# Moving fold blocks, a turned tile, the first output and the norm chain in the program order of a cross-covariance and expert kernel

## The chip, the cores and the metric

One NeuronCore of a Trainium2 chip. The metric is the device time of one execution in microseconds (us), the median of several runs. All runs quoted here were in the same undisturbed ("fast") state.

## The reference

Two stages, four batches of 6080 rows of 256:

```python
qn = q / (np.linalg.norm(q, axis=1, keepdims=True) + 1e-06)
kn = k / (np.linalg.norm(k, axis=1, keepdims=True) + 1e-06)
s = kn.transpose(0, 2, 1) @ qn / tau           # 256 x 256 per batch
a = np.exp(s - s.max(-1, keepdims=True)); a /= a.sum(-1, keepdims=True) + 1e-09
x = v @ a                                       # (24320, 256)
h = x @ w_in                                    # d_ff = 2048
r = np.maximum(h, 0.0)
out = (moe_s * (r * r) + moe_b) @ w_out
```

## The kernel before

Per batch the kernel makes a 256 x 256 matrix of scores on TensorE, divides by column norms, takes exponentials, and *folds* the result into w_in (`wa`). So h is v times `wa`, and the tokens pass through in 48 groups (47 of 512, the last of 256). A group has 16 *steps*; a step is one block of 128 hidden columns, two matmuls of 512 columns. All else is hung on a step by number (`at_step`), and every engine works strictly in that order. Between the h matmuls of group g stand the output matmuls of group g-1 (seven products in place of eight, 128 columns each), and, in batch b-1's groups, the scores and norms of batch b.

```python
# end of a batch, one item per at_step: norms (sqrt on ACT), recip (DVE: S/norm), turn (transposes),
# exps (ACT, with a table load), sums (row sums), then the folds into w_in
def scaled(f0, n, m, wa_ps):                    # half 0 on ACT, half 1 on DVE
    dst = self.wa[:, m, ds(f0, n)]
    if m == 0:
        po(nc.scalar.mul(out=dst, in_=wa_ps, mul=st["rs"][:, m : m + 1]))
    else:
        po(nc.vector.tensor_scalar_mul(out=dst, in0=wa_ps, scalar1=st["rs"][:, m : m + 1]))
# ... (cut)
if self.b == 0:
    folds = [fold_both(0, NW // 2), fold_both(NW // 2, NW // 2)]     # NW = 512
# ... (cut)
for i in range(NPIECE + 1):
    at_step(11 + i, lambda i=i: rowconst_sum(i))     # DVE sums of w_out, from DMA pieces
at_step(23, rowconst_mm)                             # ones x sums in the PSUM tile of the scores, then DVE
# ... (cut)
if g == 1:
    at_step(12, lambda g=g: transpose_v(g))          # turn v of group 1 on TensorE, copy on DVE
# ... (cut)
for b in range(1, B):
    w0 = first_group[b - 1] * FT + (26 if b == 1 else 6)      # first step of batch b's scores
    w1 = first_group[b] * FT - 3
    fin_len = 5 * 3 + 8 * 2                                   # the end starts this many steps ahead
    span = (w1 - fin_len) - w0 - 8
    n = NCH * JC                                              # 12 chunks of 4 row blocks
    for c in range(NCH):
        sc = w0 + span * c * JC / n
        # ... (cut: loads, 4 x 2 score matmuls)
        # norms of a chunk: square on ACT, square on DVE, two sums of halves on DVE
        for i, f in enumerate(ops):
            at_step(int(sc) + 2 + 1 + i * 2, f)
# ... (cut)
PLAG = {0: 14, NG - 1: 5}        # output of group 0 runs 14 steps behind its h
```

There is one PSUM tile for scores and folds, two for h, three for outputs. *rowconst* is a row that every output gets (the column sums of w_out times moe_b). Its product stands in the PSUM tile of the scores, so the first scores of batch 1 wait until DVE has read it.

Of the kernel before, what the change touches and what calls it, by code (L numbers as in the profile page):

```python
# [16 lines left out]
def kernel(  # L17
# [13 lines left out]
    P = 128  # L31

    B, N, C = q.shape
# [11 lines left out]
    CH = C // P  # L45
    FT = Dff // P
    TG = 512
    NG = (NT + TG - 1) // TG
# [5 lines left out]
    def po(ins):  # L54

        tc.keep_in_program_order(ins)
        return ins
# [30 lines left out]
    def h_tile(name):  # L88
        return ps_h.tile([P, 2, TG], FP32, tag="h_ps", name=name)
# [19 lines left out]
    class Gram:  # L109
# [105 lines left out]
        def finish_ops(self):  # L215

            st = {}

            def norms():
                self.add_norms(last=True)  # L220
                nrm = sm_pool.tile([P, 2, CH], FP32, tag="nrm", name="nrm")
                po(nc.scalar.activation(out=nrm, in_=self.n_ps, func=AF.Sqrt))  # L222
                st["nrm"] = nrm

            def recip():
                nrm = st["nrm"]
                po(nc.vector.tensor_scalar_add(out=nrm, in0=nrm, scalar1=EPS))
                st["r"] = sm_pool.tile([P, 2, CH], FP32, tag="rnrm", name="rnrm")
                po(nc.vector.reciprocal(out=st["r"], in_=nrm))
                if inv_tau != 1.0:  # L230
                    po(nc.vector.tensor_scalar_mul(
                        out=st["r"][:, 0], in0=st["r"][:, 0], scalar1=inv_tau))
                st["s"] = sm_pool.tile([P, CH, C], FP32, tag="sm_s", name="sm_s")
                po(nc.vector.tensor_mul(
                    st["s"], self.s_ps, st["r"][:, 1, :, None].broadcast_to((P, CH, C))))

            def turn():
                st["t"] = self.bank("t_ps", CH, C)
                for j in range(CH):
                    for ch in range(CH):  # L240
                        po(nc.tensor.transpose(
                            st["t"][:, j, ts(ch, P)], st["s"][:, ch, ts(j, P)], ident32))

            def exps():
                st["e"] = sm_pool.tile([P, CH, C], FP16, tag="eT", name="eT")
                for j in range(CH):
                    po(nc.scalar.activation(
                        out=st["e"][:, j, :], in_=st["t"][:, j, :], func=AF.Exp,
                        scale=st["r"][:, 0, j : j + 1]))
                self.wa = apool.tile([P, CH, Dff], FP16, tag="wa16", name="wa16")  # L250

            def sums():
                r_ps = self.bank("r_ps", CH, C)[:, :, 0]
                for ch in range(CH):
                    for j in range(CH):
                        po(nc.tensor.matmul(r_ps[:, ch : ch + 1], st["e"][:, j, ts(ch, P)],
                                            ones16[:, 0:1], start=(ch == 0 and j == 0),
                                            stop=(ch == CH - 1 and j == CH - 1),
                                            skip_group_check=True))
                st["rs"] = sm_pool.tile([P, CH], FP32, tag="rs", name="rs")  # L260
                po(nc.vector.tensor_scalar_mul(out=st["rs"], in0=r_ps, scalar1=1.0 / LAM))
                po(nc.vector.reciprocal(out=st["rs"], in_=st["rs"]))

            def scaled(f0, n, m, wa_ps):
# [4 lines that stand above are left out]
                    po(nc.vector.tensor_scalar_mul(  # L269
                        out=dst, in0=wa_ps, scalar1=st["rs"][:, m : m + 1]))  # L270

            def fold_mm(f0, n, m, wa_ps):
                for j in range(CH):
                    po(nc.tensor.matmul(wa_ps, st["e"][:, j, ts(m, P)],  # L274
                                        w_in16[:, j, ds(f0, n)],
                                        start=(j == 0), stop=(j == CH - 1)))

            def fold_both(f0, n):
                def f():
                    wa_ps = h_tile("wa_ps")  # L280
                    for m in range(CH):
                        fold_mm(f0, n, m, wa_ps[:, m, :n])
                    for m in range(CH):
                        scaled(f0, n, m, wa_ps[:, m, :n])
                return f

            def fold_one(f0, n, m):
                def f():
                    wa_ps = self.bank("wa_ps", CH, C).rearrange("p a c -> p (a c)")
                    fold_mm(f0, n, m, wa_ps)  # L290
                    scaled(f0, n, m, wa_ps)
                return f

            if self.b == 0:

                folds = [fold_both(0, NW // 2), fold_both(NW // 2, NW // 2)]
            else:
                folds = []
            folds += [fold_one(f0, NW, m) for f0 in range(NW if self.b == 0 else 0, Dff, NW)
                      for m in range(CH)]  # L300
            return [norms, recip, turn, exps, sums] + folds
# [8 lines left out]
    def group(g):  # L310
        t0 = g * TG
        return t0, min(TG, NT - t0) // P
# [3 lines left out]
    def load_v(g):  # L316
        t0, nj = group(g)
        v16 = vpool.tile([P, TG // P, C], FP16, tag="v16", name="v16")
        po(nc.gpsimd.dma_start(  # L319
            out=v16[:, :nj, :],  # L320
            in_=v_flat[t0 : t0 + nj * P, :].rearrange("(p j) c -> p j c", j=nj)))
        v_tiles[g] = v16

    def transpose_v(g):
        _, nj = group(g)
        v16 = v_tiles.pop(g)
        vT_ps = ps_h.tile([P, CH, TG], FP16, tag="h_ps", name="vT_ps")
        for j in range(nj):
            for ch in range(CH):
                po(nc.tensor.transpose(vT_ps[:, ch, ts(j, P)], v16[:, j, ts(ch, P)], ident16))  # L330
        vT = vtpool.tile([P, CH, TG], FP16, tag="vT", name="vT")
        po(nc.vector.tensor_copy(out=vT[:, :, : nj * P], in_=vT_ps[:, :, : nj * P]))
        vT_tiles[g] = vT
# [29 lines left out]
    NW = 512  # L363
# [49 lines left out]
    fin = g0.finish_ops()  # L413
# [2 lines left out]
    keep_busy(5, w_in16[:, 0, :P], w_in16[:, 0, :NW])  # L416
    fin[2]()
    transpose_v(0)
    for f in fin[3:7]:
        f()  # L420


# [32 lines left out]
    def at_step(s, f):  # L455
        side.setdefault(int(s), []).append(f)

    first_group = [b * N // TG for b in range(B)]
    for i, f in enumerate(fin[7:]):
        at_step(i // 2 * 4 + i % 2 + 1, f)  # L460
    at_step(14, lambda: po(nc.vector.tensor_scalar_mul(
        out=s_out, in0=s_bc, scalar1=1.0 / (LAM * LAM))))
    for i in range(NPIECE + 1):
# [5 lines left out]
    for g in range(NG):  # L469
        if g >= 3:  # L470
            at_step(max(g - 4, 0) * FT + 2, lambda g=g: load_v(g))
        if g >= 1:
            if g == 1:
                at_step(12, lambda g=g: transpose_v(g))
            else:
                at_step((g - 2) * FT + 6, lambda g=g: crossbar_v(g))
    for b in range(1, B):
        gr = grams[b]
        w0 = first_group[b - 1] * FT + (26 if b == 1 else 6)
        w1 = first_group[b] * FT - 3  # L480
        NCH = len(gr.chunks)
        fin_len = 5 * 3 + 8 * 2
        span = (w1 - fin_len) - w0 - 8
        n = NCH * JC
        for c in range(NCH):
            sc = w0 + span * c * JC / n
            at_step(max(3, sc - 16), lambda gr=gr, c=c: gr.load(c))
            if c == 0:
                at_step(sc, gr.start)
            for j in range(JC):  # L490
                at_step(w0 + span * (c * JC + j) / n, lambda gr=gr, c=c, j=j: gr.mm(c, j))

            def norm_step(gr=gr, c=c, sc=sc):
                ops = gr.norm_ops(c)
                for i, f in enumerate(ops):
                    at_step(int(sc) + 2 + 1 + i * 2, f)
            at_step(sc + 1, norm_step)

        def fin_step(gr=gr, s=w1 - fin_len):
            ops = gr.finish_ops()  # L500
            for i, f in enumerate(ops):
                at_step(int(s) + 1 + (i * 3 if i < 5 else 15 + (i - 5) * 2), f)
        at_step(w1 - fin_len, fin_step)
# [181 lines left out]
    work = []  # L685
    NS = NG * FT
    plain = {0, NG - 1}
    PLAG = {0: 14, NG - 1: 5}

    SQUARES = {3: (0, 1, nc.scalar), 5: (1, 2, nc.scalar), 8: (2, 4, nc.vector),  # L690
               12: (4, 6, nc.vector)}
# [1 line left out]
    for s in range(NS + FT):  # L693
        g, m = divmod(s, FT)
# [6 lines left out]
        if work:  # L701
            items, n = work[0]
# [5 lines left out]
        for gp in plain:  # L708
            mp = s - PLAG[gp] - gp * FT
            if 0 <= mp < FT:  # L710
# [47 lines left out]
```

## Time and profile before

| | before |
|---|---|
| time, median of 3 runs | 739.53 us (738.76 to 739.78) |
| span of the profiled run | 738.2 us |
| TensorE busy, matmuls | 709.0 us, 7614 |

In the profile PE is TensorE, DVE VectorE, ACT ScalarE and POOL GpSimd; the granted clock is the share of its full clock that TensorE had. The page gives the busy time of each engine; the view of waits sums TensorE's idle time by the instruction that waited and the one that released it. For the kernel before, that view (total us, count, mean us) has at its top the waits that the change aims at, on relu, on the first folds and on the turned tile:

```profile
PE h_ps L536 <- ACT r L546: 2.7, 5, 1.1
PE h_ps L536 <- DVE wa L269: 1.9, 4, 0.6
PE h_ps L536 <- DVE vT L332: 1.6, 1, 1.6
...
PE s_ps L142 <- DVE rowconst L435: 0.5, 1, 0.5
```

All these are short, and most of their time lies in the first 75 us.

### The profile page before, as it was taken

The page shows a single profiled execution, that of the slowest core. Times are in us where ns is not written, and L with a number is a line of the kernel's source. Part 1 is how long each engine was busy: PE and PEld are TensorE (multiplying, and loading weights), DVE is VectorE, ACT ScalarE, POOL GpSimd, SP SyncE. Part 2 cuts the span into 40 slices and gives each one's busy share as a digit, 9 for nine tenths or more (in the row PEclk, how much of TensorE's full clock was granted, in tenths as well). Part 3 has the DMA queues.
Part 4 walks back from the last instruction along what each step waited for, and adds up shares of the span by engine and source line. Part 5 has one row for each costly group of instructions (what it writes and reads, how often), then busy time and mean ns, then how long its engine had stood idle before and what let it go on. Part 6 is the DMA issues. An engine that isn't in the chain of part 4 may idle for free.

```text
span 738.2 us, 17834 instructions
## 1 busy us (share of the span) xinstructions
PE 709.0 (96%) x7614; PEld 510.3 (69%) x7614; DVE 625.7 (85%) x872; ACT 538.1 (73%) x573; POOL 83.3 (11%) x159
## 2 busy tenths in 40 slices
PE   4779999999999999999999999999999999999997
PEld 3535777776677777777667777777668777777776
DVE  4758999898788988988788998988878888888886
ACT  5467877787777777777778777777777777777772
POOL 4523111000111011001100111000000000000000
PEclk9999999999999999999999999999999999999999
DMA  9999988334546548323655566432322333321201
GB/s 235 209 250 155 198 153 122 73 94 94 115 98 137 136 92 152 93 68 71 129 106 123 120 125 147 99 67 64 94 66 59 72 98 76 94 58 48 77 30 73
DMA packets 83664, 80.61 MB, mean 109 GB/s; under 512 B 55712, under 2 KB 58592, under 8 KB 83584
## 3 DMA queue, kind: packets, MB, share of 16 engines
q0 software_dynamic: 23536, 40.51, 32.3%
q1 hardware_dynamic: 59616, 37.64, 18.8%
q8 instruction: 60, 0.98, 0.5%
q10 hardware_dynamic: 432, 1.31, 0.5%
q14 instruction: 20, 0.16, 0.1%
HBM read 81.00 MB, written 24.90 MB: 143 GB/s over the span
## 4 chain that ended last, share of the span: by engine, by line
PE 80%; DVE 7%; DMA 6%; ACT 4%; issue 1%; POOL 1%; DVEq 0%; POOLq 0%
PE h_ps L536 39%; PE o_ps L678 36%; PE s_ps L142 4%; ACT r L546 2%; DMA qk<-in_q_dram 2%; DMA w<-in_moe_w_out_dram 2%; DVE g L559 2%; DMA w_in<-in_moe_w_in_dram 1%; DMA qk<-in_k_dram 1%; PE wa_ps L274 1%; DVE S L604 1%; ACT g L557 1%; PE o_ps L584 1%; DVE wa L269 1%; ACT L222 1%
## 5 line engine op out<-in xcount | busy, mean ns | idle before, releaser
L546 ACT ACTIVATE r<-h_ps 128x1024 f16<-128x1024 f32 (+1 forms) x384 | 388.0, 1014 | 166.2 <-PE h_ps L536 164.1
L536 PE MATMUL h_ps<-vT,wa 128*128 128x512 f16 (+7 forms) x1632 | 453.2, 364 | 6.3 <-ACT r L546 2.7
L678 PEld LDWEIGHTS <-S 128*128 128x128 f16 x2944 | 198.1, 98 | 85.9 <-DVE S L604 1.1
L678 PEld LDWEIGHTS <-g 128*128 128x128 f16 x2208 | 155.1, 98 | 75.4 <-issue 1.2
L559 DVE TENSOR_TENSOR g<-r 128x2048 f16<-128x2048 f16 (+2 forms) x154 | 176.7, 1148 | 21.7 <-ACT r L546 21.6
L678 PE MATMUL o_ps<-T,S 128*128 128x128 f16 x2208 | 183.3, 219 | 1.0 <-DVE S L604 0.7
L536 PEld LDWEIGHTS <-wa 128*128 128x128 f16 x1632 | 136.3, 98 | 29.4 <-issue 5.7
L678 PE MATMUL o_ps<-w_out,g 128*128 128x128 f16 x1472 | 134.2, 219 | 0.0
L564 DVE SCALAR_TENSOR_TENSOR o_sb<-o_ps,s_out,u 128x256 f32<-128x256 f32 x138 | 66.4, 481 | 57.6 <-PE o_ps L678 54.2
L557 ACT ACTIVATE g<-r 128x1024 f16<-128x1024 f16 x92 | 96.7, 1051 | 0.0
L319 POOL DMA_DIRECT2D v<-in_v_dram x48 | 25.7, 537 | 534.2 <-DMA vT<-v 293.6
L142 PE MATMUL s_ps<-qk 128*128 128x256 f16 (+1 forms) x384 | 70.3, 284 | 14.2 <-ACT qk L133 7.1
L564 DVE SCALAR_TENSOR_TENSOR u<-o_ps,s_out,rowconst 128x256 f32<-128x256 f32 x138 | 65.9, 477 | 1.4 <-PE o_ps L678 1.4
L678 PE MATMUL o_ps<-N,g 128*128 128x128 f16 x736 | 63.4, 219 | 0.9 <-ACT nrm L222 0.9
L678 PE MATMUL o_ps<-w_out,S 128*128 128x128 f16 x736 | 63.4, 219 | 0.0
L165 ACT ACTIVATE sq<-qk 128x1024 f16<-128x1024 f16 (+3 forms) x49 | 50.5, 1034 | 11.8 <-DMA qk<-in_k_dram 8.7
L606 DVE TENSOR_TENSOR S<-S,g 128x2048 f16<-128x2048 f16 x46 | 56.3, 1224 | 1.3
L610 DVE TENSOR_TENSOR S<-g,S 128x2048 f16<-128x2048 f16 x46 | 55.9, 1215 | 0.0
L604 DVE TENSOR_TENSOR S<-g 128x2048 f16<-128x2048 f16 x46 | 55.9, 1214 | 0.0
L608 DVE TENSOR_TENSOR S<-g 128x2048 f16<-128x2048 f16 x46 | 55.8, 1214 | 0.0
L142 PEld LDWEIGHTS <-qk 128*128 128x128 f16 (+1 forms) x384 | 32.9, 101 | 19.7 <-DVE qk L132 9.0
L162 DVE TENSOR_TENSOR sq<-qk 128x1024 f16<-128x1024 f16 (+3 forms) x49 | 33.0, 672 | 2.6 <-DMA qk<-in_q_dram 2.6
(67 smaller groups left out, 279.0 us busy)
## 6 DMA issues: line engine op xcount, KB each, us to landing
out_dram<-o_sb SPq DMA_DIRECT2D x46, 512.0 KB, 3.0
v<-in_v_dram POOLq DMA_DIRECT2D x47, 256.0 KB, 3.9
qk<-in_k_dram POOLq DMA_DIRECT2D x42, 256.0 KB, 6.4
qk<-in_q_dram POOLq DMA_DIRECT2D x42, 256.0 KB, 7.4
vT<-v SPq DMA_TRANSPOSE x182, 2.8
w<-in_moe_w_out_dram POOLq DMA_DIRECT2D x4, 512.0 KB, 14.4
raw<-in_q_dram ACTq DMA_DIRECT2D x2, 512.0 KB, 6.7
raw<-in_k_dram SPq DMA_DIRECT2D x2, 512.0 KB, 7.0
```

What stands on the lines that cost most here:

```text
L142: po(nc.tensor.matmul(self.s_ps[:, ch, :], kc[:np_, j, ts(ch, P)], qc[:np_, j, :], start=(c == 0 and j == 0 and ch == 0), stop=(c == len(s ...
L165: po(nc.scalar.activation(out=st["sq"][:np_, 1, js, :], in_=kc[:np_, js, :], func=AF.Square))
L536: po(nc.tensor.matmul(dst, wa[:, ci, ts(m, P)], src, start=(ci == 0), stop=(ci == CH - 1), skip_group_check=True))
L546: po(nc.scalar.activation(out=r16[:, :, i % 2, :n], in_=h_tiles.pop((g, i))[:, :, :n], func=AF.Relu))
L557: po(nc.scalar.activation(out=dst, in_=src, func=AF.Square))
L559: po(nc.vector.tensor_mul(dst, src, src))
L564: po(nc.vector.scalar_tensor_tensor(out=dst, in0=src, scalar=s_out, op0=ALU.mult, in1=add, op1=ALU.add))
L604: po(nc.vector.tensor_add(S[1], A21, A22))
L606: po(nc.vector.tensor_sub(S[2], S[1], A11))
L608: po(nc.vector.tensor_sub(S[3], A11, A21))
L610: po(nc.vector.tensor_sub(S[4], A12, S[2]))
L678: po(nc.tensor.matmul(st[name][:, j, :], a()[:, i, ts(j, P)], w[:, i, :], start=first, stop=last, skip_group_check=True))
```

## The change

Its intent: start sooner (smaller first folds, folds a step sooner, group 1 turned at step 8, output of group 0 eleven steps behind), and give the work between engines more room (norm operations three steps apart instead of two, the end of a batch 38 steps ahead instead of 31).

```diff
-                folds = [fold_both(0, NW // 2), fold_both(NW // 2, NW // 2)]
+                folds = [fold_both(0, P), fold_both(P, P)]
+                folds += [fold_one(2 * P, NW - 2 * P, m) for m in range(CH)]
...
-    for f in fin[3:7]:
+    for f in fin[3:9]:
...
-    for i, f in enumerate(fin[7:]):
-        at_step(i // 2 * 4 + i % 2 + 1, f)
+    for i, f in enumerate(fin[9:]):
+        at_step(max(0, i // 2 * 4 - 1) + i % 2, f)
...
-                at_step(12, lambda g=g: transpose_v(g))
+                at_step(8, lambda g=g: transpose_v(g))
...
-        fin_len = 5 * 3 + 8 * 2
+        fin_len = 38
...
-                    at_step(int(sc) + 2 + 1 + i * 2, f)
+                    at_step(int(sc) + 2 + 1 + i * 3, f)
...
-    PLAG = {0: 14, NG - 1: 5}
+    PLAG = {0: 11, NG - 1: 5}
```

(The fold's PSUM tile is sliced to its width.) `fin_len` also enters `span`, so 38 draws the chunks of scores together, from 12 steps apart to 11.4 in batches 2 and 3, and from 9 to 8.4 in batch 1.

More of the change, by code (lines that the diff above doesn't have):

```diff
@@ L288, in f @@
                 def f():
-                    wa_ps = self.bank("wa_ps", CH, C).rearrange("p a c -> p (a c)")
+                    wa_ps = self.bank("wa_ps", CH, C).rearrange("p a c -> p (a c)")[:, :n]
                     fold_mm(f0, n, m, wa_ps)
```

## The prediction

> **What bounds the kernel now.** I read the busy shares first, then the windows view in steps of 10 us, then the timeline of TensorE with the waits ahead of its matmuls, then the timelines of DVE and ACT at the places where TensorE stood still. The page first:
>
> ```profile
> span 738.2 us, 17834 instructions
> ...
> PE 709.0 (96%) x7614; PEld 510.3 (69%) x7614; DVE 625.7 (85%) x872; ACT 538.1 (73%) x573; POOL 83.3 (11%) x159
> ```
>
> TensorE is the bound: 709.0 of 738.2 us busy, at a granted clock of 1.0. The change leaves TensorE's columns as they are (eight fold matmuls of 256 become eight of 128 and four of 256), so all it can win is idle time of TensorE: 738.2 - 709.0 = 29.2 us. The windows view tells where that is: 14.9 us before 40 us (loads of q and k, untouched), 1.08 in 40 to 50, 2.88 in 50 to 60, 0.88 in 60 to 80, nothing in 80 to 160, about 1.2 to 1.6 around each of 160-210, 350-380 and 520-560 (the ends of batches 1 to 3), 5.2 after 720 (untouched). So the change competes for about 4.8 + 4.2 = 9 us, 1.2% of the time. The stalls of the first stretch, in the timeline of TensorE (start, length, waits in brackets):
>
> ```profile
> 43.56 0.82 PE L536 MATMUL h_ps<-vT,wa 128*128 128x512 f16 x3 [0.42 <-DVE wa L269]
> ...
> 52.70 0.59 PE L536 MATMUL h_ps<-vT,wa 128*128 128x512 f16 x2 [1.11 <-ACT r L546]
> ...
> 56.15 0.59 PE L536 MATMUL h_ps<-vT,wa 128*128 128x512 f16 x2 [1.55 <-DVE vT L332]
> ...
> 66.79 0.38 PE L142 MATMUL s_ps<-qk 128*128 128x256 f16 x2 [0.50 <-DVE rowconst L435]
> ...
> 72.53 1.02 PE L536 MATMUL h_ps<-vT,wa 128*128 128x512 f16 x4 [0.37 <-ACT r L546]
> ```
>
> The 0.42 recurs at 46.89 and 50.21. DVE and ACT at that time:
>
> ```profile
> 54.27 1.23 DVE L427 TENSOR_TENSOR acc<-acc,w 128x1024 f32<-128x1024 f32 x1
> ...
> 55.41 0.68 DVE L332 COPY vT<-vT_ps 128x1024 f16<-128x1024 f16 x1
> ...
> 66.26 0.48 DVE L435 TENSOR_SCALAR rowconst<-rc_ps,b_bc 128x256 f32<-128x256 f32 x1
> ```
>
> The copy of group 1's turned tile stands on DVE behind two sums of w_out pieces, and those wait for transfers that land at 52.8 and 54.2. DVE is then busy without a gap from 52.9 to 66.7 with these sums, the combinations of the weights and rowconst. The end of a batch (batch 2):
>
> ```profile
> 352.17 0.27 PE L678 MATMUL o_ps<-N,g 128*128 128x128 f16 x2 [0.30 <-ACT nrm L222]
> ...
> 356.88 0.66 PE L241 MATMUL t_ps<-ident,sm_s 128*128 128x128 f32 x4 [0.33 <-DVE sm_s L234]
> ...
> 362.97 0.59 PE L536 MATMUL h_ps<-vT,wa 128*128 128x512 f16 x2 [0.42 <-ACT r L546]
> ...
> 369.93 0.59 PE L274 MATMUL wa_ps<-w_in,eT 128*128 128x512 f16 x2 [0.18 <-DVE wa L269]
> ```
>
> ```profile
> 359.87 1.28 ACT L247 ACT_TABLE_LOAD   x1
> 361.17 0.84 ACT L247 ACTIVATE eT<-t_ps,rnrm 128x256 f16<-128x256 f32 x2
> ```
>
> Four short stalls, 1.23 us a batch; the exponentials with their table load hold ACT for 2.1 us.
>
> **What the Trainium skill says.** "TensorE: Matmul & The Clock Gate", section "Step-by-step: what each phase is for": matmuls stay in program order, only weight loads are pulled ahead. The trace agrees: matmuls that have their data stand behind the one that waits (nothing runs in the 1.55 us before 56.15). So moving an instruction in program order is all this change does. "ScalarE: Activation LUTs", section "What ACT_TABLE_LOAD costs": about 1283 ns for a load plus about 1380 ns of drain; an ACTIVATE costs 0.833 ns an element plus a fixed part. The load is 1.28 us here, but the exponentials start 0.02 us after it and it starts 0.02 us after the relu before it, so I charge no drain. The slope agrees: the scaling of a fold takes 687 ns at 512 and 474 at 256, 0.83 ns each, so 128 wide is estimated at 0.37 us.
>
> **The change part by part.** A step is two matmuls of 512 (0.43 us). I replay the order of the changed program by hand with the durations above; TensorE's results reach ACT about 0.19 us after the issue of the last matmul ends, other hand-overs take 0.05.
>
> First fold blocks of 128. The row sums' reciprocal is there at 38.9 in both. Before: ACT 0.47, then DVE 0.48 (it waits for ACT), first h matmul at 40.03. After: 0.37 + 0.35 instead, so 39.78: **0.25 us** sooner.
>
> Folds a step or two sooner. Block 512..1023's second half is scaled by DVE behind the square of the first relu, as before, because that order is kept. The first relu now stands behind ACT's scale (0.69): it starts at 41.5 instead of 41.09, the square at 42.55, the scale ends at 43.92, TensorE's step 4 goes on at 43.97 instead of 43.56, a stall of 0.95 instead of 0.42, but with one more fold (0.43) done by then. The later two blocks come in time (45.65 for a need at 46.35, 48.65 for 50.7). Of the 3 x 0.42 two go.
>
> Group 1 turned at step 8. It runs at about 47.3; v of group 1 landed at 46.7 (issue 32.5 plus 14.2), just in time. Its copy now precedes the sums and ends at 49.2, so the **1.55 goes**. The turned tile still takes one of the two h tiles, so the wait for a relu stays: the 1.11 before 52.70 becomes some 1.2 before step 10 (49.4).
>
> First output eleven tiles behind. Its 4 matmuls of 256 a step (0.43) start at step 11 (about 50.3) instead of step 14, so TensorE is about 3 x 0.43 us of output further when it reaches step 26. There the scores of batch 1 wait for rowconst, whose PSUM tile they reuse. DVE's chain to rowconst is bound by the w_out transfers (last two at 54.2 and 55.7), not by TensorE; it only loses the copy ahead of it: 66.74 becomes 66.2. TensorE arrives there at 64.1 and stands for **2.1 us instead of 0.50**. Balance: 0.57 + 1.30 = 1.87 us won at that point. Then steps 27 to 34 have no output matmuls left, so a pair of steps is 0.87 plus 0.22 of scores, while ACT has 0.93 of relu plus the last weight casts (0.6) and a square for the norms (0.95): ACT sets the pace, two stalls of 0.4 and 0.8 instead of one of 0.37, and the relu that began at 69.59 begins at 68.62. **Left: 0.97 us**, plus 0.2 for one more pair of scores done. I take 1.1.
>
> Scores further apart, end of a batch seven steps sooner. The phases against the 16-step group move: norms 15 to 8, reciprocals 2 to 11, turn 5 to 14, exponentials 8 to 1, sums 11 to 4, folds from 14 to from 7. The norm wait (0.30) and the sm_s wait (0.33) should go, since ACT's load now fits before the norms are ready, and DVE has no S tiles in between. But the exponentials now come behind the relu of step 1: with step 1 at 0, relu ends at 1.64, load at 2.94, exponentials at 3.79; TensorE wants the sums at 3.28: **0.57**. Then ACT has relu, square, relu, square, relu, fold (five times some 0.93, then 0.69) and ends the first fold's scale at 9.0, while TensorE wants that one PSUM tile for the next fold at 8.6: **0.45**. The last fold again behind the squares of steps 3 and 5: **0.31**. Sum 1.33 against 1.23: **0.1 worse, three times 0.3**. The norm chain's operations three steps apart cost nothing themselves: TensorE has no idle in 80 to 160 and DVE is at 93% there, with batch 1's chunks 8.4 steps apart instead of 9 (101 against 108 steps for 12 chunks), so 0 to 0.4 may be lost.
>
> Sum: -1.1 + 0.3 = **-0.8 us**: 739.5 becomes 738.7.
>
> **The rivals.** One: the waits of 40 to 58 simply vanish (1.26 + 1.55 + 0.25) and so does most of a batch's end (4 x 0.3 x 3): 4 to 6 us, 734 to 735. Against it: the rowconst chain hangs on transfers, and the one h tile that the turn takes is taken in either place. Two: the moved end of a batch costs more than I count, since ACT is crowded in steps 1 to 5 (two squares, three relus, exponentials, some 6.8 us of work in 5 steps of 0.82): if each batch loses 1 us, 741. For it: ACT is already the releaser of two of the four waits; against: the two h tiles give slack, and before lost only 0.42 to the same 2.1 us. Three: v of group 1 lands later than step 8 in the changed kernel (0.6 us of margin): TensorE then waits for a transfer, some 0.5 us at most, which the rowconst wait hides anyway.
>
> **Range and chances.** The two sides that could be off are the start (won 0.8 to 2) and the ends of batches (from 0.4 won to 0.6 lost each). That gives 736.5 to 741 at the outside; for 8 in 10 I take 737.4 to 740.0. The three runs of before lie within 1.0 us. Two per cent is 14.8 us, more than all the idle the change touches, so same is nearly certain.
>
> **What would show it right or wrong.** Right: the first h matmul at 39.8; no wait on the vT copy; a wait of about 2 us of TensorE on rowconst near 66.2; two waits on relu between 69 and 72; the first matmul of group 1's output near 72.6 instead of 73.39; at each batch's end waits on the exponentials (0.5) and on fold scales, none on nrm or sm_s. Wrong: rowconst ready well before 66, matmuls of step 35 before 71.5, or stalls between 80 and 160; and a batch's end whose idle is under 0.6 or over 2 us.

## The result and the profile after

| kernel | median (lowest to highest, runs) | ratio to before, 95% |
|---|---|---|
| before, same rounds | 739.41 us (738.76 to 739.96, 6) | |
| after | 735.30 us (734.58 to 737.23, 6) | 0.9949 (0.9934 to 0.9964) |

A ratio is the mean time of one kernel's fast runs over that of the other's of the same rounds, so not quite the ratio of the medians. The change is worth 4.1 us: still "within 2%", but outside the predicted range, and the rival that named 734 to 735 was nearer. The page of the kernel after (its profiled run was the slowest of the six, 737.23 us):

```profile
span 735.5 us, 17841 instructions
...
PE 707.5 (96%) x7618; PEld 510.2 (69%) x7618; DVE 625.4 (85%) x873; ACT 537.9 (73%) x574; POOL 83.5 (11%) x159
```

TensorE's columns are the same, yet its *busy* time fell by 1.5 us although some matmuls here ran at half clock. Keep that oddity in mind. The waits of TensorE in the kernel after:

```profile
PE s_ps L142 <- DVE rowconst L436: 2.4, 1, 2.4
...
PE h_ps L537 <- DVE wa L269: 1.1, 2, 0.7
PE h_ps L537 <- DVE vT L333: 0.9, 1, 0.9
PE h_ps L537 <- ACT r L547: 0.6, 1, 0.6
```

The fold and relu waits shrank and the rowconst wait grew from 0.5 to 2.4, as predicted. In TensorE's timeline of the kernel after (start, length, waits in brackets) the start reads:

```profile
39.86 0.59 PE L537 MATMUL h_ps<-vT,wa 128*128 128x512 f16 x2 [0.39 <-DVE wa L269]
...
44.12 0.39 PE L537 MATMUL h_ps<-vT,wa 128*128 128x512 f16 x1 [0.71 <-DVE wa L269]
...
49.39 1.02 PE L537 MATMUL h_ps<-vT,wa 128*128 128x512 f16 x4 [0.95 <-DVE vT L333]
...
66.67 0.58 PE L142 MATMUL s_ps<-qk 128*128 128x256 f16 x2 [2.36 <-DVE rowconst L436]
67.05 1.91 PE L537 MATMUL h_ps<-vT,wa 128*128 128x512 f16 x4
...
73.20 0.59 PE L537 MATMUL h_ps<-vT,wa 128*128 128x512 f16 x2 [0.62 <-ACT r L547]
```

Four of these are the predicted events within 0.5 us of their places. The line at 67.05 is not: four matmuls in 1.91 us that take 1.02 elsewhere (49.39). After the 2.36 us of standing still TensorE's granted clock was 0.5 for 3.41 us, and a relu that the prediction had put at 68.62 began at 70.26.

The end of batch 2 in the same timeline, to be held against the four lines of the prediction:

```profile
344.84 0.50 PE L679 MATMUL o_ps<-T,S 128*128 128x128 f16 x6 [0.18 <-ACT nrm L222]
...
355.28 0.24 PE L256 MATMUL r_ps<-ones,eT 128*128 128x1 f16 x4 [0.41 <-ACT eT L247]
...
360.49 0.59 PE L274 MATMUL wa_ps<-w_in,eT 128*128 128x512 f16 x2 [0.41 <-ACT wa L267]
...
373.28 0.59 PE L274 MATMUL wa_ps<-w_in,eT 128*128 128x512 f16 x2 [0.17 <-ACT wa L267]
```

Four short stalls again, 1.17 us in sum against 1.23 before. By the visible stalls the ends gained next to nothing, and the start too (4.8 us of TensorE idle from 40 to 80 us before, 4.7 after, with a half clock on top). So where do 4 us come from?

**Comparing by step instead of by stall.** I took from both traces the start of the first matmul of each step; a distance between two starts needs no modelled end. Where the change gained is then plain:

| stretch of steps | before | after | gain |
|---|---|---|---|
| 0 to 64 (start, with the half clock and four more score matmuls) | 59.79 us | 61.12 us | -1.33 |
| 64 to 184 (scores and end of batch 1, four score matmuls fewer) | 113.74 | 112.30 | 1.44 |
| 184 to 384 (same, batch 2) | 184.01 | 182.77 | 1.24 |
| 384 to 576 (same, batch 3) | 175.86 | 174.61 | 1.25 |
| 576 to 760 (no scores) | 151.52 | 151.52 | 0.00 |

The three batches are 3.93 us shorter, in the place where the prediction had seen "nothing" and charged 0.3. Not all of this is a gain: with batch 1's chunks 8.4 steps apart, 38 of its score matmuls stand before step 64, with 9 steps 34. Four matmuls of 256 columns take 0.44 us, which moved from the second row of the table to the first. So **3.5 us are won** (1.0, 1.24 and 1.25), and the first row lost 0.9. Steps 64 to 576, **473.61 us before and 469.68 after**, are a sharp measure, once these 0.44 us are taken off: two kernels that differ only before step 64 agree there to 0.03 us. The start is not: kernels with the same start gave 58.4 to 59.8 us for it.

**Why the busy view did not show it.** In a dense stretch a 512-column matmul starts every 0.216 us and a 128-column one every 0.056, but each is drawn longer than that: 0.38 and 0.22 us. The Trainium skill says as much: "TensorE: Matmul & The Clock Gate", section "Wait — 56ns, not 53.3ns?", gives columns over 2.4 GHz plus about 2.5 ns (215.7 and 55.6 ns), and these traces agree; "Perfetto Trace Analysis", section "Tensor Engine Instruction (MATMUL, LD_WEIGHTS)", says that the end is estimated, "so the TE profile time is a model, not a measurement". A gap of up to 0.16 us behind a matmul is therefore covered by its drawn length and counts as busy. In the kernel before, TensorE's timeline has both kinds, first a dense pair, then one with a gap (cut from different places of its timeline):

```profile
360.61 0.22 PE L678 MATMUL o_ps<-w_out,g 128*128 128x128 f16 x1
360.66 0.59 PE L536 MATMUL h_ps<-vT,wa 128*128 128x512 f16 x2
...
272.94 0.22 PE L678 MATMUL o_ps<-w_out,g 128*128 128x128 f16 x1
273.17 0.59 PE L536 MATMUL h_ps<-vT,wa 128*128 128x512 f16 x2
```

The pair at 272.94 belongs to step 250. In TensorE's timeline of the kernel after, the same step's pair has no gap:

```profile
272.57 0.22 PE L679 MATMUL o_ps<-w_out,g 128*128 128x128 f16 x1
272.63 0.59 PE L537 MATMUL h_ps<-vT,wa 128*128 128x512 f16 x2
```

In the kernel before, the next start comes 0.05 us after a 128-column matmul in the first pair and 0.23 in the second: TensorE stood 0.18 us, and no bracket says so. Per three groups (48 steps, some 43.3 us) there were three such gaps in before, of 0.18, 0.12 and 0.01 us. "Stall by start times", below, is the distance of starts less columns / 2.4 GHz less 2.5 ns (the steady extra of one-column and fp32 matmuls, 0.02 and 0.05 us each, is left out). By it batches 2 and 3 had 0.92 us each among the scores and 2.12 at the end; after had 0.00 and 1.81. Batch 1 had 0.66 among its scores after step 64, most of it in one gap of 0.44 at step 135 that is visible in part.

### The profile page after: what moved, and what is told of

Its sections match the earlier page's. It is cut to its first block, busy times and chain, and to the rows that moved or that the text cites. A ratio compares the mean times of both kernels' runs of the same rounds, so it can differ in the third digit from the quotient of the medians.

```text
span 735.5 us, 17841 instructions
## 1 busy us (share of the span) xinstructions
PE 707.5 (96%) x7618; PEld 510.2 (69%) x7618; DVE 625.4 (85%) x873; ACT 537.9 (73%) x574; POOL 83.5 (11%) x159
## 4 chain that ended last, share of the span: by engine, by line
PE 82%; ACT 6%; DMA 6%; DVE 3%; issue 1%; POOL 1%; POOLq 0%; DVEq 0%
PE h_ps L537 40%; PE o_ps L679 36%; PE s_ps L142 4%; ACT r L547 3%; ACT g L558 2%; DMA w<-in_moe_w_out_dram 2%; DMA qk<-in_q_dram 2%; DMA w_in<-in_moe_w_in_dram 1%; DMA qk<-in_k_dram 1%; PE wa_ps L274 1%; ACT L247 1%; ACT L222 1%; POOL qk L126 1%; ACT wa L267 0%; PE o_ps L585 0%
## 5 line engine op out<-in xcount | busy, mean ns | idle before, releaser
L565 DVE SCALAR_TENSOR_TENSOR o_sb<-o_ps,s_out,u 128x256 f32<-128x256 f32 x138 | 66.5, 482 | 51.2 <-PE o_ps L679 48.9
```

The source lines that it names most:

```text
L565: po(nc.vector.scalar_tensor_tensor(out=dst, in0=src, scalar=s_out, op0=ALU.mult, in1=add, op1=ALU.add))
```

## The experiments

The theory from here on: the gain is in the score stretches and comes from the two score edits. The rivals: it comes from the start (waits that vanish), or from the ends of the batches. "Steps 64 to 576" is the duration read from the traces as above. First the change in halves.

**s_both: before with both score edits.**

```diff
-        fin_len = 5 * 3 + 8 * 2
+        fin_len = 38
-                    at_step(int(sc) + 2 + 1 + i * 2, f)
+                    at_step(int(sc) + 2 + 1 + i * 3, f)
```

> The kernel before with only the two edits of the scores (norm operations 3 steps apart, the end of a batch 38 steps ahead instead of 31). Theory 1 (from the traces of before and after: issue times of matmuls show a gain of 1.25 us in each of three batches): 3.7 us faster than before, about 735.7. Rival (the prediction): the end of a batch costs 0.1 more each, 739.5 to 740; the gain then comes from the start.

**s_start: before with all the other edits** (folds, turn, PLAG).

```diff
-                folds = [fold_both(0, NW // 2), fold_both(NW // 2, NW // 2)]
+                folds = [fold_both(0, P), fold_both(P, P)]
+                folds += [fold_one(2 * P, NW - 2 * P, m) for m in range(CH)]
... (and the later folds' steps, the turn at step 8, PLAG 11, as in the change)
```

> The kernel before with only the three edits of the start (folds, turn at step 8, output eleven tiles behind). Theory 1: 0.5 to 1.1 us faster in runs whose clock is 1.0 throughout, 738.5 to 739, and some 1.6 us slower than that, about 740, in runs in which TensorE's clock is halved for 3.4 us after the wait on rowconst. Rival: the start alone brings the 4 us, about 735.5.

**s_norm3: before with `i * 3` only.**

```diff
-                    at_step(int(sc) + 2 + 1 + i * 2, f)
+                    at_step(int(sc) + 2 + 1 + i * 3, f)
```

> The kernel before with only the norm operations 3 instead of 2 steps apart. Theory 1a (the operations' spacing takes away three gaps of 0.1 to 0.2 us every 43 us that before has among its scores): about 2.5 us faster, 737, with the four stalls at each batch's end as before. Theory 1b (the distance of the chunks, 12 steps before and 11.4 after, does it, not the spacing): the gaps stay, 739.5.

**s_finlen: before with `fin_len = 38` only.**

```diff
-        fin_len = 5 * 3 + 8 * 2
+        fin_len = 38
```

> The kernel before with only the end of a batch 38 instead of 31 steps ahead; that also sets the chunks 11.4 instead of 12 steps apart. Theory 1a: only the batch ends gain, 0.3 to 0.4 us each, about 738.4. Theory 1b: gaps among the scores go as well, about 736. Prediction: 0.1 us worse per batch, 739.8.

| kernel | median (lowest to highest) | ratio, 95% | steps 64 to 576 |
|---|---|---|---|
| before, same rounds | 739.59 us (738.8 to 741.61, 9 runs) | | 473.61 us |
| s_both | 736.27 (735.26 to 736.32) | 0.9946 (0.9933 to 0.9958) | 469.69 |
| s_start | 739.06 (738.24 to 739.97) | 0.9989 (0.9976 to 1.0001) | 473.61 |
| s_norm3 | 740.78 (740.42 to 741.54) | 1.0012 (0.9999 to 1.0026) | 474.66 |
| s_finlen | 738.64 (738.17 to 739.06) | 0.9982 (0.9969 to 0.9994) | 472.14 |

(5 runs of each variant. In the column of steps, 0.44 us of the fall of s_both and s_finlen are the four score matmuls that moved ahead of step 64; like for like s_both won 3.5 and s_finlen 1.0.) The score edits hold nearly all the gain, and their steps 64 to 576 equal those of the whole change to 0.01 us. s_norm3 met neither of its expectations (737 or 739.5). The start edits are worth 0.5 us, with an interval that reaches zero. So the rival "waits of the start vanish" falls. The page of s_both says what the busy time hid:

```profile
span 734.5 us, 17831 instructions
...
PE 705.6 (96%) x7614; PEld 508.9 (69%) x7614; DVE 625.1 (85%) x872; ACT 537.9 (73%) x573; POOL 83.3 (11%) x159
```

The same 7614 matmuls were "busy" 709.0 us before and 705.6 here: those 3.4 us were gaps drawn as work. In the windows view (columns PE, PEld, DVE, ACT, POOL with their instructions, granted clock, DMA share, GB/s) of the kernel before, then of s_both, the 130 us inside batch 2's scores look alike:

```profile
210.00:340.00 130.00, 129.96 (x1421) 94.91 (x1419) 117.65 (x162) 99.18 (x103) 13.27 (x25) 1.00 0.51 106
```

```profile
210.00:340.00 130.00, 130.00 (x1427) 95.14 (x1425) 118.27 (x163) 99.91 (x104) 13.26 (x25) 1.00 0.54 109
```

Idle of 0.04 and of 0.00 us; the six more matmuls in the second are what shows.

The two halves do not add: `i * 3` alone costs 1.0 us of steps 64 to 576 and `fin_len` alone wins 1.0 (without the moved matmuls), together they win 3.5. `fin_len` does two things, though: it moves the end, and it draws the chunks together. The next two runs part them.

**b_span: before with `i * 3` and chunks 11.4 steps apart, the end left at 31.**

```diff
-                    at_step(int(sc) + 2 + 1 + i * 2, f)
+                    at_step(int(sc) + 2 + 1 + i * 3, f)
-        span = (w1 - fin_len) - w0 - 8
+        span = (w1 - 38) - w0 - 8
```

> The kernel before with the norm operations 3 steps apart and the chunks 11.4 steps apart, but each batch's end where it was (31 steps ahead). Theory (the gaps among the scores and the batch's end are two separate gains): the gaps are gone, 0 instead of 0.91 us a batch, the batch's end still loses 2.1 us; 2 to 2.5 us faster than before, 737 to 737.6. Rival (the gain comes from the place of the batch's end alone): 739.5.

**b_finonly: before with the end at 38, chunks still 12 steps apart, `i * 2`.**

```diff
-        fin_len = 5 * 3 + 8 * 2
+        fin_len = 38
-        span = (w1 - fin_len) - w0 - 8
+        span = (w1 - 31) - w0 - 8
```

> The kernel before with the batch's end 38 steps ahead, chunks still 12 steps and norm operations 2 steps apart. Theory: the gaps of 0.91 us a batch stay, the batch's end loses 1.8 instead of 2.1 (first batch 2.7); 0.9 to 1.5 us faster, 738 to 738.7. Rival: nothing, 739.5.

| kernel | median (lowest to highest, 5 runs) | ratio, 95% | steps 64 to 576 | stall by start times, batches 2 and 3: scores / end |
|---|---|---|---|---|
| before, same rounds | 739.63 us (738.64 to 740.23, 9 runs) | | 473.61 us | 0.92 / 2.12 |
| b_span | 737.10 (736.81 to 738.00) | 0.9969 (0.9957 to 0.9982) | 470.76 | 0.00 / 2.12 |
| b_finonly | 737.59 (736.53 to 738.41) | 0.9972 (0.9958 to 0.9985) | 471.64 | 0.92 / 1.59 |
| s_norm3 | | | 474.66 | 1.37 / 2.33 |
| s_finlen | | | 472.14 | 0.98 / 1.92 |
| s_both (after: 469.68) | | | 469.69 | 0.00 / 1.81 |

The fall of 2.85 us in b_span contains the 0.44 us of moved matmuls. So of 3.5 us, **2.4 come from spacing 3 together with chunks 11.4 (8.4 in batch 1) apart**, which leaves no gap among the scores (0.92 + 0.92 + 0.66 before), and 1.08 more come with the moved end. The medians agree with this count: 3.3 us for 3.5 (s_both), 2.5 for 2.4 (b_span), 2.0 for 2.0 (b_finonly), 0.95 for 1.0 (s_finlen). Neither spacing 3 with chunks 12 apart (s_norm3) nor spacing 2 with chunks 11.4 apart (s_finlen) removes the gaps. The moved end by itself wins 1.97, so the two parts overlap by 0.9: with the end moved, an end on the old chunks stalls 1.59, one on the new chunks 1.81.

What exactly collides? In the view of all engines of the kernel before, ACT stands like this beside one of the 0.18 us gaps (start, length):

```profile
226.94 1.06 ACT L557 ACTIVATE g<-r 128x1024 f16<-128x1024 f16 x1
227.88 1.05 ACT L165 ACTIVATE sq<-qk 128x1024 f16<-128x1024 f16 x1
228.83 1.94 ACT L546 ACTIVATE r<-h_ps 128x1024 f16<-128x1024 f32 x2
```

A norm square (sq) directly behind a regular square (g) puts the relus a microsecond back, and h has only two PSUM tiles. If that neighbourhood, at step 5 of a group, were the whole cause, moving the scores by one step should remove the gap.

**b_phase: before with the scores of batches 2 and 3 one step sooner.**

```diff
-        w0 = first_group[b - 1] * FT + (26 if b == 1 else 6)
+        w0 = first_group[b - 1] * FT + (26 if b == 1 else 5)
```

> The kernel before with the scores of batches 2 and 3 begun one step sooner, so that no chunk's square of k falls on ACT at step 5 of a group, next to ACT's second square of the main work. Theory (that coincidence makes the gaps of 0.18 us at step 10): those three gaps per batch are gone; gaps of DVE at other steps may stay; among the scores of a batch 0.2 to 0.7 us stand instead of 0.91; time 738.5 to 739.5. Rival (the gaps have another cause): 0.18 at step 10 stays.

740.22 us (739.99 to 741.21, 4 runs), ratio 1.0011 (0.9998 to 1.0024) to before's 739.60 (738.34 to 739.85, 12 runs); steps 64 to 576 grew by 1.21 us, the gaps among the scores from 0.92 to 1.52 in each of batches 2 and 3. The gap at step 10 of a group stayed and another of 0.22 us came at step 7. My explanation by the one neighbour is refuted. That the gaps depend on the *phase* of the norm chain against the 16-step group is what the settings show (0.92, 0.98, 1.37, 1.52, 0.00), b_phase most directly, which moved the chain by one step alone; which pair of instructions makes each gap stays open.

Now the start, where the rowconst wait and the half clock stood.

**a_fill: after with nine dummy 512-column matmuls in the rowconst wait.**

```diff
+    def fill_wait():
+        z_ps = ps_o.tile([P, 2, C], FP32, tag="o_ps", name="z_ps").rearrange("p j c -> p (j c)")
+        for _ in range(9):
+            po(nc.tensor.matmul(z_ps, w_in16[:, 0, :P], w_in16[:, 0, :NW], start=True, stop=True, skip_group_check=True))
...
             if c == 0:
+                if b == 1:
+                    at_step(sc, fill_wait)
                 at_step(sc, gr.start)
```

> The changed kernel with nine matmuls of 512 whose result nobody reads (1.94 us), put ahead of the first scores of batch 1, into TensorE's wait of 2.4 us on rowconst. Theory (the wait halves the clock for 3.4 us in some runs): no half clock after the wait in any run, the runs close together near the fastest of the changed kernel, about 734.6, instead of 734.6 to 737.2. Rival (the halved clock comes from elsewhere, or the spread is noise): the same spread, or slower, since more is issued.

**a_rc21: after with the rowconst product two steps sooner.**

```diff
-    at_step(23, rowconst_mm)
+    at_step(21, rowconst_mm)
```

> The changed kernel with rowconst's matmul and scaling two steps sooner (step 21), so that on DVE it stands ahead of the last combination of weights (1.7 us). Theory: the wait of the first scores of batch 1 shrinks from 2.4 to about 0.7 us plus 0.5 at step 21 for the sum that isn't ready, the clock stays at 1.0, and since ACT sets the pace in steps 27 to 34 no more than 1 us of it is kept: 734 to 734.6. Rival: the wait is hidden behind ACT altogether, 735.3 as before.

**a_w30: after with the scores of batch 1 from step 30 instead of 26**, so that the wait for rowconst falls where it has already ended.

```diff
-        w0 = first_group[b - 1] * FT + (26 if b == 1 else 6)
+        w0 = first_group[b - 1] * FT + (30 if b == 1 else 6)
```

> The changed kernel with the scores of batch 1 begun at step 30 instead of 26, so that TensorE reaches them after rowconst is there. Theory: no wait on rowconst, steps 26 to 30 run on, ACT sets the pace there; clock at 1.0; 0.5 to 1.5 us faster than the changed kernel's median, 734 to 734.8. Rival: the chunks of batch 1, closer now (8.1 steps), bring gaps of their own and the time stays at 735.3 or grows.

**a_lag14: after with PLAG back at 14.**

```diff
-    PLAG = {0: 11, NG - 1: 5}
+    PLAG = {0: 14, NG - 1: 5}
```

> The changed kernel with the first output fourteen tiles behind again. Theory (the prediction's replay: 1.3 us of output done ahead of the wait on rowconst, of which ACT's pace takes back some): the wait on rowconst shrinks by 0.8 to 1.3 us, the clock stays at 1.0, and the time is within 1 us of the changed kernel: 734.5 to 736. Rival: the lag is what the start lives from, 737 or more.

| kernel | median (lowest to highest, runs) | ratio, 95% |
|---|---|---|
| before, same rounds | 739.63 us (739.12 to 739.85, 11) | |
| a_fill | 735.24 (735.11 to 735.42, 5) | 0.9941 (0.9929 to 0.9953) |
| a_rc21 | 733.45 (733.35 to 734.74, 5) | 0.9922 (0.9910 to 0.9934) |
| a_w30 | 733.12 (732.79 to 734.49, 4) | 0.9916 (0.9903 to 0.9929) |
| a_lag14 | 735.79 (735.01 to 738.84, 6) | 0.9954 (0.9939 to 0.9968) |

The rowconst wait was worth about 2 us: two different ways round it (a_rc21, a_w30) both give that, each more than its expectation had allowed (734 at best), so ACT did not hold back as much as I thought. TensorE's timeline of a_w30 shows no wait at the scores and only two short ones on relu:

```profile
65.94 0.59 PE L537 MATMUL h_ps<-vT,wa 128*128 128x512 f16 x2 [0.25 <-ACT r L547]
66.37 0.38 PE L142 MATMUL s_ps<-qk 128*128 128x256 f16 x2
...
67.62 0.59 PE L537 MATMUL h_ps<-vT,wa 128*128 128x512 f16 x2 [0.44 <-ACT r L547]
```

The clock is told apart by the windows view from 60 to 70 us (granted clock third from the end) of after, then of a_fill:

```profile
60.00:70.00 10.00, 7.64 (x40) 4.29 (x39) 9.49 (x20) 6.49 (x13) 5.31 (x10) 0.83 1.02 135
```

```profile
60.00:70.00 10.00, 9.69 (x58) 5.52 (x56) 9.14 (x18) 7.92 (x15) 5.82 (x11) 1.00 0.97 146
```

With the wait filled the clock stays at 1.0 and the runs lie within 0.3 us, but the median is that of after (735.24 against 735.30). What the filler can take away is a tail: two of after's six runs stood at 736.85 and 737.23, and the profiled 737.23 is one in which the clock halved. The run at 736.85 has the lowest mean granted clock of the six, 0.996. The half clock that stands at the end of the profiled runs lasts at most 2.5 us, which leaves a mean of 0.998; 0.996 is some 5 to 6.6 us at half clock (an estimate from the rounded mean), so it very likely halved there too. A mean of 0.998 does not tell: the profiled run has it, and so have the two fastest. No run of a_fill has less than 0.998.

a_lag14 was a miss: I had expected a shorter rowconst wait with the later output. TensorE's timeline of a_lag14 has a longer one, and its clock halved too:

```profile
66.12 0.38 PE L142 MATMUL s_ps<-qk 128*128 128x256 f16 x2 [2.98 <-DVE rowconst L436]
```

With less output done TensorE comes there sooner (63.1 us against 64.3) and waits for the same chain; the output is then still to do. The median ended 0.5 us behind that of after, within the spread of both.

**a_turn12: after with group 1 turned at step 12 as before.**

```diff
-                at_step(8, lambda g=g: transpose_v(g))
+                at_step(12, lambda g=g: transpose_v(g))
```

> The changed kernel with group 1 turned at step 12 again. Theory (all of the start before step 26 is paid back at the wait on rowconst): the wait on the vT copy, about 1.5 us, is back, the wait on rowconst shrinks by as much, rowconst itself comes 0.5 us later since the copy is ahead of it on DVE; no halved clock; 735 to 736. Rival: the 1.5 us come off the whole time, 736.8.

735.77 us (734.89 to 737.18, 4 runs), ratio 0.9949 (0.9935 to 0.9963). TensorE's timeline of a_turn12:

```profile
56.15 0.59 PE L537 MATMUL h_ps<-vT,wa 128*128 128x512 f16 x2 [1.87 <-DVE vT L333]
...
66.79 0.38 PE L142 MATMUL s_ps<-qk 128*128 128x256 f16 x2 [0.49 <-DVE rowconst L436]
```

The 1.87 us on the turned tile are back and the rowconst wait falls from 2.36 to 0.49: the same time is lost in either place. That is why this part of the change won almost nothing.

**a_fold_late: after with the later folds at their old steps.**

```diff
-        at_step(max(0, i // 2 * 4 - 1) + i % 2, f)
+        at_step(i // 2 * 4 + i % 2 + 1, f)
```

> The changed kernel with the 512-wide folds at their old steps. Theory: the stalls of steps 4, 8 and 12 are as in the kernel before (0.7 each with the part the profile hides), TensorE reaches rowconst later and waits less; the time stays within 0.5 us of the changed kernel, 734.6 to 735.8. Rival: it is slower by the two stalls that the change took away, 736.2.

734.91 us (734.70 to 735.46, 4 runs), ratio 0.9938 (0.9925 to 0.9951): not slower than after. Folds a step sooner win nothing while the rowconst wait follows. In this run that wait was 1.72 us, and the clock stayed at 1.0 until the end of the span:

```profile
66.14 0.38 PE L142 MATMUL s_ps<-qk 128*128 128x256 f16 x2 [1.72 <-DVE rowconst L436]
```

Last, two attempts to go further from a_w30 at the ends of the batches.

**a_w30_fin: row sums four steps behind the exponentials, folds three steps later.**

```diff
-            at_step(int(s) + 1 + (i * 3 if i < 5 else 15 + (i - 5) * 2), f)
+            at_step(int(s) + 1 + ((0, 3, 6, 9, 13)[i] if i < 5 else 18 + (i - 5) * 2), f)
```

> The changed kernel with the scores of batch 1 begun at step 30 and, at each batch's end, the row sums 4 instead of 3 steps behind the exponentials and the folds 2 steps later. Theory (the exponentials end 0.5 us after TensorE wants the row sums, and ACT's backlog behind them delays the first fold's scale): the two stalls of 0.57 us go, those of 0.34 on the norms and about 0.3 on a late fold stay; 0.8 to 1.1 us a batch, 3 us in all: 730 to 730.8. Rival: ACT's backlog shifts onto an h tile, and no more than 1 us is won, 732.

**a_w30_f42: the end 42 steps ahead, chunks as with 38.**

```diff
-        fin_len = 38
+        fin_len = 42
-        span = (w1 - fin_len) - w0 - 8
+        span = (w1 - 38) - w0 - 8
```

> The changed kernel with the scores of batch 1 begun at step 30 and each batch's end four steps sooner still (exponentials at step 13 of a group instead of 1, chunks as they are). Theory (the exponentials cost what ACT's two squares at steps 3 and 5 leave no room for): away from those squares the batch's end loses 0.8 to 1.4 us instead of 1.8; 731.3 to 732.5. Rival: the same 1.8 us wherever it stands, 733.1.

a_w30_fin gave 733.25 us (732.70 to 733.60, 4 runs), ratio 0.9914 (0.9901 to 0.9926); a_w30_f42 gave 733.32 (733.22 to 734.00, 5 runs), ratio 0.9919 (0.9906 to 0.9931). Both equal a_w30, and the end of a batch still stalls 1.80 and 1.76 us by start times. The waits only change their names; in a_w30_fin the sums wait no longer, and TensorE's timeline has a relu in their place, behind the same table load and exponentials on ACT:

```profile
176.26 0.59 PE L537 MATMUL h_ps<-vT,wa 128*128 128x512 f16 x2 [0.42 <-ACT r L547]
```

My expectation that shifting the steps saves 0.8 to 1.1 us is refuted. The end of batch 2 or 3 stalls 1.6 to 2.3 us in every variant run; the lowest, 1.59, is b_finonly's.

The best version is a_w30, 733.12 us, ahead of both kernels (a_rc21 and the two last runs lie within 0.4 us of it, so the choice among these is not shown).

## Why the prediction was right or wrong

**The start: right in events, one thing missed.** First h at 39.86 (predicted 39.8; the folds of 128). One fold stall of 0.71 us ending at 44.12 (0.95 at 43.97), the two others gone. The copy's 1.55 gone; a stall of 0.95 at 49.39 (1.2 at 49.4, though the profile names the turned tile and not the relu). The rowconst wait 2.36 us at 66.67 (2.1 at 66.2); the first w_out sum, which waits for its transfer, came 0.46 us later than in before, and the chain kept the delay. What no step foresaw is that the clock halves after that wait: in the profiled run, with the longer wait, it turned the predicted gain of 1.1 into a loss of 0.9 by start times (1.33 less the 0.44 of moved scores). Over the runs the start edits are worth 0.5 us of median (s_start), so the term was of the right kind and too large; 735.30 against 736.27 of s_both, from other rounds, gives 1.0. In the profile of s_start the rowconst wait was 1.16 us, the clock stayed at 1.0 there, and the two predicted relu stalls are there:

```profile
65.47 0.38 PE L142 MATMUL s_ps<-qk 128*128 128x256 f16 x2 [1.16 <-DVE rowconst L436]
...
68.91 0.59 PE L537 MATMUL h_ps<-vT,wa 128*128 128x512 f16 x2 [0.28 <-ACT r L547]
...
70.77 1.02 PE L537 MATMUL h_ps<-vT,wa 128*128 128x512 f16 x4 [0.62 <-ACT r L547]
```

By start times that profile won 1.6 us in steps 0 to 64. So without the half clock the start went much as worked out, though rowconst came 1.2 us sooner there than in after; one profile each.

**The sentence that failed: "The norm chain's operations three steps apart cost nothing themselves: TensorE has no idle in 80 to 160", with "0 to 0.4 may be lost".** The idle was there: b_span won 2.4 us over the three batches (2.85 by steps, less 0.44 of matmuls that moved): 0.92 in each of batches 2 and 3 from gaps under 0.2 us that the drawn lengths of matmuls cover almost wholly, and 0.66 in batch 1. It was not checked by start times, though the skill's warning that ends are modelled stood ready. Because of the same reading, the sentence "all it can win is idle time of TensorE: 738.2 - 709.0 = 29.2 us" set the wrong frame: s_both's gain came out of the 709.0. And the listed sign of error, "stalls between 80 and 160", looked at the one batch with few of these gaps (0.11 us in steps 64 to 130, the other 0.55 just past the window at 166 and 168 us; 0.92 in batches 2 and 3) and in a view that could not show them.

**The ends of the batches: the term of +0.1 a batch was -0.36.** The list of waits was nearly right: 0.41, 0.41 and 0.17 visible on exponentials and fold scales (predicted 0.57, 0.45, 0.31), and only the norm wait was wrongly called gone (0.18). What failed is comparing predicted full waits with the visible 1.23 of before. By start times before lost 2.12 there, not 1.23, and after 1.81. The predicted 1.33 was set against the wrong number. Of the 1.08 us of the three ends only the difference between b_span and s_both speaks, so it contains whatever the chunks' new places did to it.

**The rivals.** One named the right time for the wrong reason: the start's waits did not vanish (s_start, a_turn12), and the visible stalls of the ends hardly fell. Two, a dearer end, is refuted; with the end moved each was cheaper. Three, a late v of group 1, did not show: the stall at 49.39 is 0.95 and no transfer is named.

**The sum.** Predicted -1.1 + 0.3 = -0.8. Measured: start about -0.5 (s_start), scores -2.4, ends -1.1, together -4.0, against -4.1 by the medians of after. So close an agreement is partly luck, since the start is known to some 0.5 us only and the runs of after with a halved clock are in that median.

**Open.** Which pair of instructions makes each hidden gap; why a moved end and new chunks overlap by 0.9 us; whether a third PSUM tile for h would close the gaps whatever the phase (no run tried it); how often the clock halves without a profile.

## What to carry to other kernels

Before you say that the bounding engine has no idle time, compare starts with the pitch that dense stretches of the same trace show, or compare the busy time of two kernels with the same matmuls: a fall of busy time means that gaps were in it. If you compare a stretch between two steps, count its matmuls too: here 0.44 of 3.93 us were work that had moved out of the stretch. When periodic side work (here a norm chain every 12 steps) runs beside a loop of another period (16), try two or three spacings *together with* the period, since one alone can lose what both win. And a stall moved ahead of a wait that hangs on a transfer is only handed on to it: move the waiting instruction (a_rc21, a_w30) before you polish what comes ahead.

## What the Trainium skill lacked or had wrong

- "TensorE: Matmul & The Clock Gate", section "HAM oscillation — how this bites in real kernels": its rule is no gap of TensorE over about 3.4 us. Here gaps of 2.36 (after) and 2.98 us (a_lag14) in an otherwise busy stretch were followed by 3.41 us at half clock; gaps of 1.16 (s_start), 1.72 (a_fold_late) and 1.87 us (a_turn12) were not, nor was anything in the kernels with the gap filled or removed (a_fill, a_rc21, a_w30). One profile each. By these profiles the rule is too lenient. In both the clock fell 51.2 us, 15 times 3.41, after it had first risen (at the end of the gap in after, 0.5 us behind it in a_lag14), so where a gap lies against such stretches may count beside its length; no run tested that. The length at half clock agrees with the window that the page gives (3413 ns).
- "Perfetto Trace Analysis", section "Tensor Engine Instruction (MATMUL, LD_WEIGHTS)": right that the end is modelled, but neither it nor that page's warning against matmul busy time as a measure says how much idle time that hides. Here gaps up to 0.16 us behind any matmul counted as busy, 0.92 us in one batch's scores and 3.4 us of busy time in a whole kernel.
- "ScalarE: Activation LUTs", section "What ACT_TABLE_LOAD costs": the load's 1283 ns agree (1.28 us), the drain of about 1380 ns did not show (0.02 us on either side of the load).
- No page covers periodic side work whose phase against the main loop decides small stalls: 0.92, 0.98, 1.37, 1.52 and 0.00 us a batch for five settings of the same instructions.
